# Sharing one PSUM bank between modulation columns and a K tile, an earlier normalisation, and a last tile in four pieces, in a transformer block on one core

## Chip, cores, metric

The kernel runs on one core of a Trainium2 chip (the runs came from several chips; each kernel ran next to the kernel before on the same chip). The metric is the device time of one execution in microseconds (us), the median of several runs. One run with the hardware profiler gives the trace; the span that the trace shows (first to last instruction) is about 1.8 us shorter than the time of the same run. Engines: PE multiplies matrices, PEld loads its weights, DVE and ACT work on vectors, POOL does small things, SP issues the DMAs. PSUM is the memory in which PE sums its products; this kernel uses it as eight banks of 512 columns.

## The reference

One transformer block on 2048 tokens of width 1024, cut to what matters here:

```python
mod = (silu(c) @ w_mod).reshape(1, 6, 1, -1)          # six modulation vectors from one condition vector
sa, ca, ga, sb, cb, gb = ...
h = layernorm(x) * (1 + ca) + sa                      # first modulation: needs sa and ca as columns
x = x + ga * linear_attention(h, wqkv, wo)            # q, k, v = h @ wqkv, 32 heads
h = layernorm(x) * (1 + cb) + sb
x = x + gb * ((gelu(h @ w_gate) * (h @ w_up)) @ w_down)
```

## The kernel before

Instructions are recorded in program order per engine, and semaphore waits are derived from byte ranges. Only two places matter.

The **head** is the first 39 us: nothing can be multiplied before x, the modulation weights and the K weights arrive. The first four token chunks (128 tokens each; below "first" to "fourth tokens") are normalised on DVE and transposed on PE. The modulation columns for a quarter of the width (two of the eight 128-wide slices `dc`) come from 32 one-column matmuls; DVE copies them out of PSUM and applies them; then that quarter of the K product can run. K of four chunks has eight tiles (chunk, half `jg`), each a sum of eight matmuls in a PSUM bank of its own. Seven banks are in `kb0`. The eighth tile (chunk 3, half 1) has bank 4, in which the columns are also made, so it may start only after the last copy.

```python
def mod_cols(q, bank, copy=True):                     # 4 columns, 8 matmuls each
    ...                                               # columns q*4 .. q*4+3 of the bank, start=(dc == 0)
    if copy: mod_copy(q, bank)                        # DVE: columns PSUM -> SBUF

kb0 = {(0, 0): 0, (0, 1): 1, (1, 0): 2, (1, 1): 3, (2, 0): 5, (2, 1): 6, (3, 0): 7}
...
mod_cols(0, 4, False); ...; mod_copy(0, 4); mod1(0, 1, 0, 2)   # mod1(c0, n, dc0, dc1): apply on DVE
warm(4, 7)                                            # matmuls of zeros, while waiting
k_part(0, [0])                                        # quarter 0, first tokens
ln1_bn(3, 0); mod1(1, 1, 0, 2)
k_part(0, [1])
xhat_dve(2, *xh_buf(2)); t1(2, 7)                     # third tokens: normalise, transpose, ACT copy
ln1_bn(3, 1); ln1_fin(3); mod1(2, 1, 0, 2)
warm(5)
k_part(0, [2])
xhat_dve(3, *xh_buf(3)); mod_cols(1, 4); mod1(0, 3, 2, 4); t1(3, 7)
k_part(1, [0, 1, 2]); mod1(3, 1, 0, 4); k_part(0, [3])
mod_cols(2, 4); mod1(0, 4, 4, 6)
k_part(1, [3])                                        # runs while DVE copies and applies the third columns
warm(1)
k_part(2, [0, 1, 2])
mod_cols(3, 4); mod1(0, 4, 6, 8)
k_part(2, [3])                                        # these 2 and
kv_mm(3, "k", 1, 4, list(range(6)))                   # these 6 run while DVE copies and applies the fourth
for (c_, jg), b in kb0.items():
    kv_mm(c_, "k", jg, b, [6, 7])
kv_mm(3, "k", 1, 4, [6, 7])
...                                                   # then V: (chunk, half) in the order (0,0) (1,0) | (0,1) (1,1) | ...
```

The **tail** is the last output tile. Each piece is 28 matmuls, two DVE steps and an output DMA:

```python
for k, (c0, c1) in enumerate(((0, 512), (512, 896), (896, 1024)) if last_tile else ((0, 512), (512, 1024))):
```

## Time and profile before

| what | value | where |
|---|---|---|
| time | 838.89 us, median of 3 (838.37 to 840.59); the profiled run 839.12 | times |
| span, PE busy | 837.3 us, 99% | page |
| granted clock | 1.000 | cores view |
| first columns to first V matmul ("K stage") | 9.73 to 31.46: 21.73 us | timeline of PE |
| last DVE step to end of span | 835.32 to 837.3 us | timeline |

The page of the kernel before: the span, the busy times, the clock in 40 slices, and the chain of work that ended last, by engine.

```profile
span 837.3 us, 11206 instructions
...
PE 825.8 (99%) x4081; PEld 383.3 (46%) x4160; DVE 511.5 (61%) x893; ACT 336.1 (40%) x555; POOL 37.1 (4%) x91
...
PEclk9999999999999999999999999999999999999999
...
PE 91%; DMA 4%; ACT 1%; DVE 1%; SPq 1%; issue 1%; POOL 0%; ACTq 0%; POOLq 0%
```

PE is nearly always busy and holds 91% of the chain, at full clock, so a change of order like this one can gain only at the edges of the span. The timeline of PE in the head, kernel before. Columns: start, length, engine, line, operation, names, shapes, count, and in brackets the idle time before it and what ended it. L600 makes modulation columns, L546 transposes, L680 is K (`wk`) and V (`wv`), L736 is warm-up. (A 512-wide matmul is recorded as 0.379 us long, and the next one starts 0.216 us after it; so a group's length includes 0.16 us in which its last matmul drains.)

```profile
9.73 0.95 PE L600 MATMUL ps_all<-siluT,wmq 128*128 128x1 bf16 x32 [1.33 <-DMA wmq<-in_w_mod_dram]
...
13.62 0.61 PE L546 MATMUL ps_all<-ident,xh 128*128 128x128 bf16 x8
14.06 1.24 PE L736 MATMUL ps_all<-warm 128*128 128x512 bf16 x5
15.70 1.04 PE L680 MATMUL ps_all<-wk,h1T 128*128 128x512 bf16 x4 [0.39 <-DVE h1T L565]
16.57 0.94 PE L600 MATMUL ps_all<-siluT,wmq 128*128 128x1 bf16 x32
...
21.22 0.94 PE L600 MATMUL ps_all<-siluT,wmq 128*128 128x1 bf16 x32
...
22.90 2.75 PE L680 MATMUL ps_all<-wk,h1T 128*128 128x512 bf16 x11
25.48 0.94 PE L600 MATMUL ps_all<-siluT,wmq 128*128 128x1 bf16 x32
26.29 5.34 PE L680 MATMUL ps_all<-wk,h1T 128*128 128x512 bf16 x23
31.46 3.62 PE L680 MATMUL ps_all<-wv,h1T 128*128 128x512 bf16 x16
35.46 3.61 PE L680 MATMUL ps_all<-wv,h1T 128*128 128x512 bf16 x16 [0.38 <-issue]
```

Four groups of columns start at 9.73, 16.57, 21.22 and 25.48, so the K stage has four segments, each from one group to the next: 6.84, 4.65, 4.26 and 5.98 us. Transposes of the third tokens come at 13.62, after the second tokens' K matmuls, and then PE has nothing useful until 15.70. The second V half begins at 35.46 after a wait of 0.38 us, counted from the end of the drain before it. The chain of waits of the same kernel, in order of time (start, length, what; a piece starts where the one before it ends, so here 0.17 us later than in the timeline):

```profile
25.65 0.78 PE ps_all L600 x32
26.43 1.53 PE ps_all L680 x7
...
35.08 0.38 issue
35.46 0.59 PE ps_all L680 x2
```

The tail in the timeline of DVE, kernel before: the last two pieces, 384 and 128 wide.

```profile
833.13 0.57 DVE L1135 TENSOR_TENSOR ps_all<-ps_all,gbb 128x384 f32<-128x384 f32 x1 [3.12 <-PE ps_all L1130]
...
834.69 0.30 DVE L1135 TENSOR_TENSOR ps_all<-ps_all,gbb 128x128 f32<-128x128 f32 x1 [0.41 <-PE ps_all L1130]
835.03 0.29 DVE L1137 TENSOR_TENSOR xall<-ps_all,xall 128x128 bf16<-128x128 f32 x1
```

### The profile page before, as it was taken

To read this page: it belongs to the slowest core of one execution; us is meant where nothing else is said; L and a number is where in the kernel's file an instruction comes from. 1 tells how busy PE (TensorE), PEld (TensorE's weight loads), DVE (VectorE), ACT (ScalarE), POOL (GpSimd) and SP (SyncE) were. 2 spreads that over 40 slices of the span, in tenths; PEclk is the share of its full clock that TensorE was granted. 3 is DMA by queue.
4 is the path that set the end of the run, shared out by engine and by line. 5 is a ranking of instruction groups with operands and counts; after the bars stand their busy time and mean duration, and the time that the engine had idled before them with its cause. 6 is when DMAs were issued, how large, how long until landed. Compare 5 with 4: busy or idle time off the path is not lost.

```text
span 837.3 us, 11206 instructions
## 1 busy us (share of the span) xinstructions
PE 825.8 (99%) x4081; PEld 383.3 (46%) x4160; DVE 511.5 (61%) x893; ACT 336.1 (40%) x555; POOL 37.1 (4%) x91
## 2 busy tenths in 40 slices
PE   7999999999999999999999999999999999999998
PEld 4444444444444444444444444444444444444444
DVE  6678877687785577753455665356656535655512
ACT  2357777446423354420355442045554104445300
POOL 2011111000200000010000000000000000000000
PEclk9999999999999999999999999999999999999999
DMA  9994322239696769180555533055553305555000
GB/s 286 315 253 93 109 76 74 80 81 234 145 227 207 220 203 276 30 195 26 158 151 151 151 101 75 20 158 151 151 151 101 76 20 160 153 153 144 7 19 26
DMA packets 183942, 113.22 MB, mean 135 GB/s; under 512 B 35400, under 2 KB 174920, under 8 KB 182864
## 3 DMA queue, kind: packets, MB, share of 16 engines
q1 hardware_dynamic: 183872, 112.50, 49.6%
q8 instruction: 33, 0.54, 0.3%
q14 instruction: 21, 0.17, 0.1%
q10 hardware_dynamic: 16, 0.00, 0.0%
HBM read 100.67 MB, written 4.47 MB: 126 GB/s over the span
## 4 chain that ended last, share of the span: by engine, by line
PE 91%; DMA 4%; ACT 1%; DVE 1%; SPq 1%; issue 1%; POOL 0%; ACTq 0%; POOLq 0%
PE ps_all L1130 23%; PE ps_all L1105 23%; PE ps_all L1102 21%; PE ps_all L680 13%; PE ps_all L721 7%; PE ps_all L1045 2%; DMA wu<-in_B_w_up_dram 1%; DMA h2T<-xh 1%; PE ps_all L702 1%; DMA wmq<-in_w_mod_dram 1%; DMA scr_rd<-rdc 1%; DMA rb<-scr_rd 1%; SPq L978 0%; PE ps_all L947 0%; PE ps_all L600 0%
## 5 line engine op out<-in xcount | busy, mean ns | idle before, releaser
L1105 PE MATMUL ps_all<-h2T,wu 128*128 128x512 bf16 x896 | 339.6, 379 | 1.9
L1102 PE MATMUL ps_all<-h2T,wg 128*128 128x512 bf16 x860 | 325.9, 379 | 0.0
L1130 PE MATMUL ps_all<-wd,yT 128*128 128x512 bf16 (+2 forms) x906 | 193.0, 372 | 0.9
L1113 ACT ACTIVATE q<-ps_all 128x512 f32<-128x512 f32 x112 | 66.9, 597 | 226.2 <-PE ps_all L1102 218.9
L1130 PEld LDWEIGHTS ps_all<-wd,yT 128*128 128x128 bf16 x924 | 89.2, 98 | 104.7 <-issue 0.4
L1102 PEld LDWEIGHTS ps_all<-h2T,wg 128*128 128x128 bf16 x896 | 87.7, 98 | 105.8 <-issue 0.2
L1105 PEld LDWEIGHTS ps_all<-h2T,wu 128*128 128x128 bf16 x896 | 87.7, 98 | 105.6
L1118 DVE SCALAR_TENSOR_TENSOR ww<-th,guh 128x512 f32<-128x512 f32 x112 | 77.5, 692 | 77.9 <-ACT th L1117 77.9
L1115 DVE SCALAR_TENSOR_TENSOR ww<-q,ps_all 128x512 f32<-128x512 f32 x112 | 76.9, 687 | 77.5 <-ACT guh L1114 77.4
L1117 ACT ACTIVATE th<-ww 128x512 f32<-128x512 f32 x112 | 70.5, 629 | 87.3 <-DVE ww L1115 87.3
L1135 DVE TENSOR_TENSOR ps_all<-ps_all,gbb 128x512 f32<-128x512 f32 (+2 forms) x33 | 22.5, 682 | 95.2 <-PE ps_all L1130 95.2
L1120 DVE TENSOR_TENSOR yT<-ww,ps_all 128x512 bf16<-128x512 f32 x112 | 76.9, 687 | 3.8
L1114 ACT ACTIVATE guh<-ps_all 128x512 f32<-128x512 f32 x112 | 66.3, 592 | 0.0
L680 PE MATMUL ps_all<-wk,h1T 128*128 128x512 bf16 x252 | 57.8, 379 | 1.0 <-DVE h1T L565 0.8
L680 PE MATMUL ps_all<-wv,h1T 128*128 128x512 bf16 x255 | 57.6, 379 | 0.4 <-issue 0.4
L669 ACT ACTIVATE eb<-ps_all 128x512 f32<-128x512 f32 x64 | 37.4, 600 | 48.9 <-PE ps_all L721 23.2
L721 PE MATMUL ps_all<-h1T,wq 128*128 128x512 bf16 x243 | 56.2, 379 | 0.7
L1045 PE MATMUL ps_all<-w,pq 128*128 128x512 bf16 x251 | 56.0, 379 | 0.3
L670 DVE TENSOR_SCALAR eb<-eb 128x512 f32<-128x512 f32 x64 | 27.1, 424 | 27.2 <-ACT eb L669 26.9
L1045 PEld LDWEIGHTS ps_all<-w,pq 128*128 128x128 bf16 x256 | 25.0, 98 | 30.1 <-issue 0.2
L680 PEld LDWEIGHTS ps_all<-wv,h1T 128*128 128x128 bf16 x256 | 24.9, 98 | 30.3 <-DVE eb L670 0.8
L680 PEld LDWEIGHTS ps_all<-wk,h1T 128*128 128x128 bf16 x256 | 24.5, 98 | 30.8 <-DVE h1T L565 2.3
(94 smaller groups left out, 477.1 us busy)
## 6 DMA issues: line engine op xcount, KB each, us to landing
wg<-in_B_w_gate_dram SPq DMA_DIRECT2D x56, 512.0 KB, 4.1
wu<-in_B_w_up_dram SPq DMA_DIRECT2D x56, 512.0 KB, 5.2
rb<-scr_rd SPq DMA_DIRECT2D x32, 256.0 KB, 6.9
wd<-in_B_w_down_dram SPq DMA_DIRECT2D x7, 1024.0 KB, 9.1
wmst<-in_w_mod_dram SPq DMA_DIRECT2D x6, 1024.0 KB, 6.7
wmq<-in_w_mod_dram SPq DMA_DIRECT2D x8, 512.0 KB, 7.7
out_dram<-xall SPq DMA_DIRECT2D x31, 128.0 KB, 1.7
xall<-in_A_x_dram SPq DMA_DIRECT2D x3, 1024.0 KB, 12.5
```

The lines of the kernel that those rows point to most:

```text
L680: o = sch.op(T, lambda e, dc=dc: e.matmul(PS(bank), H1[sg][:, dc, ci * P:(ci + 1) * P], W_[:, dc, jg * 512:(jg + 1) * 512], start=(dc == 0 ...
L721: o = sch.op(T, lambda e, dc=dc: e.matmul(PS(b), WQ[:, dc, qc * P:(qc + 1) * P], H1[sg][:, dc, :], start=(dc == 0), stop=(dc == NDC - 1)), ...
L1045: last[half] = sch.op(T, lambda e, g=g, half=half: e.matmul(PS(b0 + half), PQ[sg][:, g, ci * P:(ci + 1) * P], W2[:, g, half * 512:(half + ...
L1102: og = sch.op(T, lambda e, dc=dc: e.matmul(PS(bg), WG[slot][:, dc, e_ * P:(e_ + 1) * P], H2[sg][:, dc, :], start=(dc == 0), stop=(dc == ND ...
L1105: ou = sch.op(T, lambda e, dc=dc: e.matmul(PS(bu), WU[slot][:, dc, e_ * P:(e_ + 1) * P], H2[sg][:, dc, :], start=(dc == 0), stop=(dc == ND ...
L1113: sch.op(A, lambda e: e.activation(Q1[j][:, :], PS(bg), ACTF.Square, scale=math.sqrt(GELU_A)), prd=pr(bg), wr=rq, note=f"q1 {fc}")
L1114: ogh = sch.op(A, lambda e: e.activation(GUH[j][:, :], PS(bg), ACTF.Copy, scale=0.5), prd=pr(bg), wr=rg, note=f"gh {fc}")
L1115: sch.op(V, lambda e: e.scalar_tensor_tensor(WW[j][:, :], Q1[j][:, :], 1.0, PS(bg), op0=ALU.add, op1=ALU.mult), rd=rq, prd=pr(bg), wr=rw, ...
L1117: sch.op(A, lambda e: e.activation(TH[j][:, :], WW[j][:, :], ACTF.Tanh, scale=GELU_C), rd=rw, wr=rt, note=f"th {fc}")
L1118: sch.op(V, lambda e: e.scalar_tensor_tensor(WW[j][:, :], TH[j][:, :], 1.0, GUH[j][:, :], op0=ALU.add, op1=ALU.mult), rd=rt + rg, wr=rw, n ...
L1120: sch.op(V, lambda e: e.tensor_tensor(YT[:, fc, :], WW[j][:, :], PS(bu), ALU.mult), rd=rw, prd=pr(bu), wr=r_yt(fc), note=f"yT {fc}")
L1130: o = sch.op(T, lambda e, b=b, fc=fc, c0=c0, c1=c1, n=n: e.matmul(PS(b, 0, n), YT[:, fc, ci * P:(ci + 1) * P], WDT[fc // 4][:, fc % 4, c0:c1],
```

## The change

Its intent: (1) put the 16 modulation columns at the end of bank 4, so that the eighth K tile can accumulate in columns 0 to 495 of the same bank from the first quarter on (its last 16 columns come at the end, as eight 128x16 matmuls); (2) move the third tokens' normalisation and transposes ahead of the second tokens' K matmuls; (3) finer last pieces, for a shorter tail. The third-quarter K weights are also split into two loads. Core of the diff:

```diff
-            for d0, d1 in ((2 * q, 2 * q + 2),) if q < 3 else ((6, 7), (7, 8)):
+            for d0, d1 in ((2, 4),) if q == 1 else ((2 * q, 2 * q + 1), (2 * q + 1, 2 * q + 2)):
...
+        MC0 = 496                      # columns now at MC0 + q * 4 ...
-                            start=(dc == 0), stop=(dc == NDC - 1)),
+                            start=(q == t == b == dc == 0), stop=(dc == NDC - 1), skip_group_check=True),
...
+        def k31(dcs, c0=0, c1=MC0):    # eighth tile, columns c0..c1 of bank 4, start only for c0 > 0
...
         k_part(0, [0])
-        ln1_bn(3, 0)
-        mod1(1, 1, 0, 2)
-        k_part(0, [1])
         xhat_dve(2, *xh_buf(2))
         t1(2, 7)
+        mod1(1, 1, 0, 2)
+        ln1_bn(3, 0)
         ln1_bn(3, 1)
         ln1_fin(3)
+        k_part(0, [1])
         mod1(2, 1, 0, 2)
-        warm(5)
+        warm(2)
...
         k_part(0, [3])                 # k_part(q, [3]) now includes k31 of that quarter
+        k_part(1, [3])
         mod_cols(2, 4)
+        mod_copy(2, 4)
+        warm(2)
         mod1(0, 4, 4, 6)
-        k_part(1, [3])
-        warm(1)
-        k_part(2, [0, 1, 2])
+        k_part(2, [0, 1, 2, 3])
         mod_cols(3, 4)
+        mod_copy(3, 4)
         mod1(0, 4, 6, 8)
-        k_part(2, [3])
-        kv_mm(3, "k", 1, 4, list(range(6)))
         for (c_, jg), b in kb0.items():
             kv_mm(c_, "k", jg, b, [6, 7])
-        kv_mm(3, "k", 1, 4, [6, 7])
+        k31([6, 7])
+        k31(list(range(NDC)), MC0, 512)
...
-            ... ((0, 512), (512, 896), (896, 1024)) if c_ == NCH - 1 ...
+            ... ((0, 512), (512, 832), (832, 960), (960, 1024)) if c_ == NCH - 1 ...
```

More of the change, by code (lines that the diff above doesn't have):

```diff
@@ L590, in mod2, with mod_cols @@
             mods(H2, r_h2, sg, sc2, ci * P, (ci + n) * P, 0, NDC, "h2")
-        def mod_cols(q, bank, copy=True):
+        MC0 = 496
+        def mod_cols(q, bank):
             o = None
-            rng = [(bank * 2048 + q * 16, bank * 2048 + (q + 1) * 16)]
+            rng = [(bank * 2048 + (MC0 + q * 4) * 4, bank * 2048 + (MC0 + q * 4 + 4) * 4)]
             for t in range(2):
                 for b in range(2):
-                    col = q * 4 + t * 2 + b
+                    col = MC0 + q * 4 + t * 2 + b
                     for dc in range(NDC):
@@ L605, in mod_cols @@
                 sch.ps.set_writer(t_[0], t_[1], o)
-            if copy:
-                mod_copy(q, bank)
         def mod_copy(q, bank):
-            rng = [(bank * 2048 + q * 16, bank * 2048 + (q + 1) * 16)]
-            sch.op(V, lambda e: e.tensor_tensor(MODT[:, q * 4:q * 4 + 4], PS(bank, q * 4, q * 4 + 4), ADD4[:, :], ALU.add),
+            rng = [(bank * 2048 + (MC0 + q * 4) * 4, bank * 2048 + (MC0 + q * 4 + 4) * 4)]
+            sch.op(V, lambda e: e.tensor_tensor(MODT[:, q * 4:q * 4 + 4], PS(bank, MC0 + q * 4, MC0 + q * 4 + 4), ADD4[:, :], ALU.add),
                    prd=rng, rd=r_sm("add4"), wr=r_smc("modt", q, 16), note=f"modcp{q}")
@@ L751, in bass_adaLN_cond__linear_attn_block__geglu_ffn__prompt_kernel, with k_part @@
         kb0 = {(0, 0): 0, (0, 1): 1, (1, 0): 2, (1, 1): 3, (2, 0): 5, (2, 1): 6, (3, 0): 7}
-        def k_part(q, cs, dcs=(0, 1)):
-            for dc in [2 * q + k for k in dcs]:
+        def k31(dcs, c0=0, c1=MC0):
+            rng = [(4 * 2048 + c0 * 4, 4 * 2048 + c1 * 4)]
+            for dc in dcs:
+                o = sch.op(T, lambda e, dc=dc: e.matmul(PS(4, c0, c1), H1[0][:, dc, 3 * P:4 * P], WK[:, dc, 512 + c0:512 + c1],
+                                                        start=(c0 > 0 and dc == 0), stop=(dc == NDC - 1), skip_group_check=True),
+                           rd=r_h1(0, dc, dc + 1, 3 * P, 4 * P) + r_w(OFF_WK, "wk", dc, 512 + c0, 512 + c1),
+                           pwr=(rng if dc == 0 else ()), note=f"k c3 jg1 dc{dc} {c0}")
+            if dcs[-1] == NDC - 1:
+                sch.ps.set_writer(*rng[0], o)
+        def k_part(q, cs):
+            for dc in (2 * q, 2 * q + 1):
                 for (c_, jg), b in kb0.items():
@@ L757, in k_part @@
                         kv_mm(c_, "k", jg, b, [dc])
+                if 3 in cs:
+                    k31([dc])
         warm(11, 7)
@@ L769, in bass_adaLN_cond__linear_attn_block__geglu_ffn__prompt_kernel @@
         warm(6, 7)
-        mod_cols(0, 4, False)
+        mod_cols(0, 4)
         ln1_bn(2, 0)
@@ L791, in bass_adaLN_cond__linear_attn_block__geglu_ffn__prompt_kernel @@
         mod_cols(1, 4)
+        mod_copy(1, 4)
+        t1(3, 7)
         mod1(0, 3, 2, 4)
-        t1(3, 7)
         k_part(1, [0, 1, 2])
@@ L1124, in ffn_down @@
             db = 6 if ci % 2 == 0 else 4
-            for k, (c0, c1) in enumerate(((0, 512), (512, 896), (896, 1024)) if c_ == NCH - 1 else ((0, 512), (512, 1024))):
-                b = db + k if k < 2 else 0
+            for k, (c0, c1) in enumerate(((0, 512), (512, 832), (832, 960), (960, 1024)) if c_ == NCH - 1 else ((0, 512), (512, 1024))):
+                b = db + k if k < 2 else k - 2
                 n = c1 - c0
```

## The prediction

> **What bounds the kernel now.** The page gives PE 825.8 us busy of an 837.3 us span (99%), granted clock 1.000. In the chain of waits PE is 91%. After 35.5 us the timeline of PE runs to 834.67 us without a hole that this change touches. So only the first 35 us and the last 3 us are open.
>
> *Head.* The timeline shows useful PE work between 9.73 us (first modulation columns) and 31.46 us (first V matmul): 64 K matmuls at 0.216 us (13.8), 4 column groups at 0.79 (3.2), 3 token transposes at 0.46 (1.4): 18.4 us. The other 3.3 us are warm-up matmuls and waits: about 0.9 before the first K matmul, 1.5 at 14.2 to 15.7 us (third tokens late: ACT copy 1.03, then DVE), 0.5 before 18.43, 0.5 before 22.9. But DMA is at 9 tenths throughout, and landings follow each other by bytes: third and fourth columns' weights at 21.4 and 25.6 us, last K weights 26.9, the second half of the V weights about 35.4 us (issued 24.1, 11.2 us to landing). The PE wait of 0.38 us that ends at 35.46, listed as "issue", is this last DMA: PE could have gone on at 35.08.
>
> *Tail.* PE ends at 834.67; then DVE 0.31 + 0.29, then about 2 us of output DMA.
>
> **What the change does, costed.**
> - Third tokens' normalisation, transposes and ACT copy move up in front of the second tokens' K matmuls: third tokens' K matmuls start at about 14.8 instead of 15.70: -0.9 us there; three warm-ups fewer, one more later.
> - The eighth K tile loses its wait for all column copies, so it runs by quarters. It adds eight 128x16 matmuls; the 1-column ones went at 25 to 30 ns each, so +0.2 us.
> - The fourth columns now come after all third-quarter K matmuls (PE about 26.3 to 27.1, no DMA wait left), but nothing is left to fill the copy (0.16) and modulation (first piece 0.35): about 0.5 us bare wait that before was filled with eight matmuls. Roughly 0.2 to 0.6 bare before the third quarter remains.
> - Summed: K stage ends about 31.1 instead of 31.46, -0.3 us. Then PE needs the second V half: at 34.7 instead of 35.08, and still gets it at about 35.4. The bytes ahead of it are the same and splitting one weight DMA takes none away. So the 0.3 us turn into a longer wait for that DMA (0.38 to about 0.7): head gain 0, unless the landing moves.
> - Tail: pieces of 384+128 took 4.55+1.56 us; 320+128+64 take 3.80+1.56+0.81 = +0.06 us (slope 0.42 ns per column between the two forms). The Trainium skill, "TensorE: Matmul & The Clock Gate", section "Wait — 56ns, not 53.3ns?", gives 55.6 ns at 128 columns, and a floor of about 25 ns; this trace has 55.7 ns and no 64-column form. The last two DVE steps shrink from 0.30 to about 0.23 each (1.05 ns per column): -0.14. Output DMA unchanged. Net -0.1 us.
>
> **Prediction.** 838.6 us, 837.8 to 839.5; faster by 2% 0.5%, within 2% 99%, slower 0.5%.
>
> **What would show it.** Timeline of PE: third tokens' K at about 14.8; first V matmul at about 31.1; second-half V still at 35.4 with a longer wait; from there the same spacing to the end; last DVE steps near 0.23; PE end to span end about 0.1 shorter.
>
> **What would make it wrong.** The second V half landing earlier (then up to 0.6 us gain) or later (the extra DMA shifts which DMA each later issue waits for; then a loss); a column group waiting for its weights now that PE comes earlier; 64-column matmuls slower than 29 ns because weight loads no longer hide; 128-byte output rows landing later.

## More of the kernel before

L702 is the first K-V product, which needs V of the first tokens.

After the fourth columns (25.48) K matmuls follow at once (26.29).

## The result

The changed kernel took 838.88 us (median of 6, 838.56 to 839.24); the kernel before, on the same chip, 838.38 (median of 6, 838.08 to 840.59). The ratio is 1.0002, 95% interval 0.9989 to 1.0014. Ratios here are the mean time of one kernel's fast runs over that of the other's in the same rounds, so not quite the ratio of the medians. The kernel before now and then takes 839.9 to 840.7 us (5 of the 39 of its runs), and those pull its mean up. Three of the five list a mean granted clock of 0.998 instead of 1.000, which by itself would make 0.002 x 838.6 = 1.7 us; one (839.90) lists 1.000, and for one (840.59) no clock is on record. Medians are the better guide below: 838.60 over those 39 runs, 839.08 over 11 runs of the changed kernel (6 here, 5 in a repeat). The changed kernel is about 0.5 us, or 0.06%, slower. The interval of the ratio includes 1, in the repeat too (0.9993 to 1.0018), so this rests on the medians and on the traces below.

The page of the changed kernel, the lines that answer to those before:

```profile
span 836.8 us, 11359 instructions
...
PE 830.2 (99%) x4194; PEld 384.4 (46%) x4194; DVE 511.7 (61%) x895; ACT 336.1 (40%) x555; POOL 37.1 (4%) x91
...
PE 98%; DMA 1%; DVE 1%; SPq 0%; ACT 0%; issue 0%
```

The span of this profiled run is 0.5 us shorter than that of the profiled run before, while the medians go the other way. One profile each is not enough for half a microsecond. (No reading rests on PE's share of the chain, 91% and 98%: it is 97% in a second profile of the kernel before.) The timeline of PE, changed kernel (L602 makes columns, L756 is the eighth tile):

```profile
9.20 0.95 PE L602 MATMUL ps_all<-siluT,wmq 128*128 128x1 bf16 x32 [0.59 <-DMA wmq<-in_w_mod_dram]
...
14.27 1.04 PE L680 MATMUL ps_all<-wk,h1T 128*128 128x512 bf16 x4 [0.17 <-DVE h1T L565]
15.14 0.94 PE L602 MATMUL ps_all<-siluT,wmq 128*128 128x1 bf16 x32
...
21.06 0.94 PE L602 MATMUL ps_all<-siluT,wmq 128*128 128x1 bf16 x32
21.86 0.59 PE L736 MATMUL ps_all<-warm 128*128 128x512 bf16 x2
22.71 1.69 PE L680 MATMUL ps_all<-wk,h1T 128*128 128x512 bf16 x7 [0.25 <-DVE h1T L565]
...
26.16 0.94 PE L602 MATMUL ps_all<-siluT,wmq 128*128 128x1 bf16 x32
27.81 3.30 PE L680 MATMUL ps_all<-wk,h1T 128*128 128x512 bf16 x14 [0.71 <-DVE h1T L565]
...
31.57 7.07 PE L680 MATMUL ps_all<-wv,h1T 128*128 128x512 bf16 x32
38.47 0.62 PE L702 MATMUL ps_all<-vs,pk 128*128 128x129 bf16 x8
```

The third tokens' K matmuls (14.27) come 5.07 us after the first columns instead of 5.97: the gain of 0.9 us is there. But the third columns start at 21.06 and the third-quarter K matmuls only at 22.71, and the fourth columns start at 26.16 and the fourth-quarter matmuls at 27.81. The segments are 5.94, 5.92, 5.10 and 5.41: 22.37 us, 0.64 more than before. The first V matmul starts at 31.57, although the first columns came 0.53 us earlier in this execution. From there 32 V matmuls run without a wait for the second V half. The chain of waits behind the fourth columns, changed kernel:

```profile
26.32 0.79 PE ps_all L602 x32
...
27.14 0.17 DVE modt L611
...
27.34 0.42 DVE h1T L565
...
27.81 3.30 PE ps_all L680 x14
```

Before, K matmuls stood at this place in the chain. Now the chain leaves PE for the copy (0.17) and the first application (0.42). Seen from PE, it issues nothing useful from 26.95 (26.16 plus 32 column matmuls, 0.79) to 27.81: 0.86 us. Those are 0.16 of drain, 0.17 of copy, 0.42 of application, and 0.1 of hand-overs.

The tail of the changed kernel, DVE:

```profile
831.95 0.50 DVE L1149 TENSOR_TENSOR ps_all<-ps_all,gbb 128x320 f32<-128x320 f32 x1 [2.38 <-PE ps_all L1144]
...
834.33 0.23 DVE L1149 TENSOR_TENSOR ps_all<-ps_all,gbb 128x64 f32<-128x64 f32 x1 [0.19 <-PE ps_all L1144]
834.59 0.23 DVE L1151 TENSOR_TENSOR xall<-ps_all,xall 128x64 bf16<-128x64 f32 x1
```

The last two DVE steps take 0.23 us instead of 0.30 and 0.29.

### The profile page after: what moved, and what is told of

Its sections match the earlier page's. It is cut to its first block, busy times and chain, and to the rows that moved or that the text cites. A ratio compares the mean times of both kernels' runs of the same rounds, so it can differ in the third digit from the quotient of the medians.

```text
span 836.8 us, 11359 instructions
## 1 busy us (share of the span) xinstructions
PE 830.2 (99%) x4194; PEld 384.4 (46%) x4194; DVE 511.7 (61%) x895; ACT 336.1 (40%) x555; POOL 37.1 (4%) x91
## 3 DMA queue, kind: packets, MB, share of 16 engines
HBM read 100.67 MB, written 4.47 MB: 126 GB/s over the span
## 4 chain that ended last, share of the span: by engine, by line
PE 98%; DMA 1%; DVE 1%; SPq 0%; ACT 0%; issue 0%
PE ps_all L1144 23%; PE ps_all L1116 23%; PE ps_all L1119 23%; PE ps_all L680 13%; PE ps_all L1059 7%; PE ps_all L721 7%; PE ps_all L702 1%; DMA wmq<-in_w_mod_dram 1%; PE ps_all L961 0%; PE ps_all L602 0%; DVE h1T L565 0%; PE ps_all L973 0%; PE ps_all L756 0%; PE ps_all L643 0%; SPq L442 0%; DVE st L742 0%
## 5 line engine op out<-in xcount | busy, mean ns | idle before, releaser
L1116 PE MATMUL ps_all<-h2T,wg 128*128 128x512 bf16 x896 | 339.6, 379 | 0.0
L1144 PE MATMUL ps_all<-wd,yT 128*128 128x512 bf16 (+3 forms) x952 | 194.2, 366 | 0.0
L1149 DVE TENSOR_TENSOR ps_all<-ps_all,gbb 128x512 f32<-128x512 f32 (+3 forms) x34 | 22.7, 667 | 94.8 <-PE ps_all L1144 94.8
L721 PE MATMUL ps_all<-h1T,wq 128*128 128x512 bf16 x256 | 58.7, 379 | 0.0
```

Of the source, the lines that this page charges most:

```text
L721: o = sch.op(T, lambda e, dc=dc: e.matmul(PS(b), WQ[:, dc, qc * P:(qc + 1) * P], H1[sg][:, dc, :], start=(dc == 0), stop=(dc == NDC - 1)), ...
L1116: og = sch.op(T, lambda e, dc=dc: e.matmul(PS(bg), WG[slot][:, dc, e_ * P:(e_ + 1) * P], H2[sg][:, dc, :], start=(dc == 0), stop=(dc == ND ...
L1144: o = sch.op(T, lambda e, b=b, fc=fc, c0=c0, c1=c1, n=n: e.matmul(PS(b, 0, n), YT[:, fc, ci * P:(ci + 1) * P], WDT[fc // 4][:, fc % 4, c0:c1],
```

## The experiments

Two theories at the start. **A**: the order of work on PE sets the time of the head; the changed kernel lost its filler behind the third and fourth columns, and the 0.38 us wait in the profile before was one execution's late load. **B** (that of the prediction): the second V half's DMA sets the time of both. A third, **D**, comes up with the parts: the weight DMAs pace the columns, so an earlier PE only waits for them. Each kernel ran five times or six, next to the kernel before on the same chip, with one profile each. All outputs were correct.

The segments in all profiles, in us. "V asked" is when PE would start on the second V half (first V matmul plus 16 x 0.216); "V landed" is from the landing records of the trace. Both are on the clock of the span.

| kernel | 1st to 2nd columns | to 3rd | to 4th | to first V | K stage | V landed / asked | median time (before beside it) |
|---|---|---|---|---|---|---|---|
| before | 6.84 | 4.65 | 4.26 | 5.98 | 21.73 | 35.4 / 34.9 | 838.89 |
| before again | 6.84 | 4.65 | 4.25 | 5.98 | 21.72 | 31.9 / 34.8 | 838.60 (838.61) |
| changed | 5.94 | 5.92 | 5.10 | 5.41 | 22.37 | 34.0 / 35.0 | 838.88 (838.38) |
| changed again | 5.98 | 5.92 | 5.09 | 5.42 | 22.41 | 32.6 / 35.6 | 839.18 (838.61) |
| tail only | 6.88 | 4.65 | 4.35 | 5.98 | 21.86 | 33.8 / 34.8 | 838.80 (838.61) |
| third tokens up only | 5.97 | 4.65 | 4.47 | 5.98 | 21.07 | 33.7 / 34.5 | 838.07 (838.62) |
| eighth tile only | 6.83 | 5.91 | 5.10 | 5.40 | 23.24 | 33.3 / 36.4 | 840.06 (838.62) |
| filler behind 4th columns | 6.58 | 5.91 | 4.24 | 5.41 | 22.14 | 32.9 / 35.1 | 838.34 (838.61) |
| filler behind 3rd and 4th | 5.97 | 5.49 | 4.23 | 5.41 | 21.10 | 32.8 / 33.7 | 837.58 (838.62) |
| the same again | 6.92 | 5.49 | 4.23 | 5.41 | 22.05 | 32.9 / 35.5 | 838.10 (838.58) |
| all but the eighth tile | 5.97 | 4.65 | 4.24 | 5.98 | 20.84 | 32.0 / 34.0 | 837.65 (838.58) |
| third tokens, tail, V order | 5.97 | 4.65 | 4.90 | 5.98 | 21.51 | 33.2 / 36.2 | 838.66 (838.62) |
| before, late V half | 6.85 | 4.64 | 4.25 | 5.98 | 21.72 | 35.7 / 35.3 | 839.66 (838.53) |
| changed, late V half | 6.08 | 5.92 | 5.09 | 5.41 | 22.50 | 35.7 / 35.7 | 839.60 (838.53) |

The two odd first segments (6.58, 6.92) belong to executions in which the first K weights landed late: the first K matmul came 2.76 and 3.11 us after the first columns, instead of 2.14 to 2.27 in the other rows. In both, the landing records have these weights 0.14 us before that matmul (12.10 and 12.96 us). (For the version with another V order, "asked" is eight matmuls later.)

From the first V matmul to the end of the span, the profiles without a wait in the V stage agree: 805.31 us with three tail pieces, 805.21 to 805.22 with four (times from the packed trace, which has three decimals). So the span is the start of the first columns, the K stage, and this constant. The first columns start when their weights land, and that differs between executions of one kernel (9.73 and 9.65 us before, 9.20 and 9.76 changed). This is why K stages can be compared between single profiles and whole spans can't.

### Both kernels again

> The kernel before, unchanged, against itself: ratio 1.000, and its spread is the noise of the comparison. Theory A (the PE order sets the time; the profile of before fell on an execution with late weights): the second V half lands at about 34 us as in the profile after, the first V matmul starts at about 31 and no wait stands before the second V half; span about 836.6. Theory B (the second V half's DMA sets the time of both kernels): it lands at about 35.4 again and PE waits for it again.

> The changed kernel, unchanged. Theory A: the K stage, from the first modulation columns to the first V matmul, takes about 22.4 us again, 0.6 more than in before (21.7), no wait for the second V half, and the time is 0.3 to 0.6 us above before. Theory B: the time equals before within 0.1, and the second V half lands when PE asks for it or later.

The kernel before, repeated: the timeline of PE at the start of V.

```profile
31.37 7.07 PE L680 MATMUL ps_all<-wv,h1T 128*128 128x512 bf16 x32
38.27 0.62 PE L702 MATMUL ps_all<-vs,pk 128*128 128x129 bf16 x8
```

The 32 V matmuls run through: 6.90 us from the first V matmul to the first K-V product, against 7.45 in the first profile, so there the late load cost 0.55 us (the 0.38 idle and the 0.16 of drain). The second V half had landed at 31.9. Before took 838.60 (838.61 beside it), the changed kernel 839.18. Theory A's numbers hold (K stage 21.72 and 22.41, difference 0.69, time 0.57). In this pair both kernels found the load landed, so theory B can't set the difference.

### The tail alone

```diff
-  ... ((0, 512), (512, 896), (896, 1024)) if c_ == NCH - 1 ...
+  ... ((0, 512), (512, 832), (832, 960), (960, 1024)) if c_ == NCH - 1 ...
```

> The kernel before with only the last output tile in four pieces. By the costs read from the trace: PE end 0.06 us later, last two DVE steps 0.14 shorter: 0.1 us faster than before, the head unchanged. Rival: the tail is what costs the 0.4 us (smaller output rows land later): then this kernel is 0.3 to 0.5 us slower than before, and the time from the last DVE step to the end of the span grows.

The time (838.80 against 838.61) is too coarse for 0.1 us, and its sign was missed. The trace resolves it: from the first K-V product to the end of the last DVE step 796.35 us, against 796.41 in both profiles of before; from there to the end of the span 1.97, against 2.00 in both. The tail gains 0.10 us, as expected, and the rival (smaller output rows cost 0.4) falls.

### Filler behind the fourth columns

The first build put the eighth tile's matmuls behind the fourth columns as filler, as the kernel before had done (there they come after two matmuls of another bank and wait for the copy). PE would write bank 4 while DVE reads the columns out of it, and nothing orders the two. The Trainium skill, "PSUM — Partial Sum Buffer", section "PSUM bank collisions raise a hardware error", says why this counts even with disjoint columns: two engines may not touch one bank in the same 32 partitions at once. No run here shows it. So the filler was taken from tiles in other banks:

```diff
-        k_part(2, [0, 1, 2, 3])
+        k_some(2, [(0, 0), (0, 1), (1, 0), (1, 1), (2, 0)])
+        k31([4, 5])
         mod_cols(3, 4)
         mod_copy(3, 4)
+        k_some(2, [(2, 1), (3, 0)])
         mod1(0, 4, 6, 8)
```

> The changed kernel with four third-quarter K matmuls (tiles that are not in the shared bank) moved from in front of the fourth columns to behind them, so that PE has work while the columns are copied and applied. Theory A: the bare 0.7 us before the fourth-quarter matmuls goes, first V matmul 0.7 us earlier relative to the first columns, and the time falls by 0.6 to 0.7 us against the changed kernel. Theory B: the 0.7 us reappear as a wait before the second V half and the time is that of the changed kernel within 0.15.

```profile
26.20 0.94 PE L602 MATMUL ps_all<-siluT,wmq 128*128 128x1 bf16 x32
27.00 4.15 PE L680 MATMUL ps_all<-wk,h1T 128*128 128x512 bf16 x17
```

In the timeline of PE the 17 K matmuls recorded after the fourth columns (26.20) start at once (27.00). The third segment falls by 0.85 us, from 5.09 to 4.24 (four matmuls moved out of it), and the fourth stays at 5.41, since the four now stand where PE had been idle. The K stage of this profile fell by only 0.27 because its first K weights landed late. The time fell by 0.84, from 839.18 to 838.34, somewhat more than the 0.6 to 0.7 that A expected. B expected no change.

### The parts alone

Third tokens moved up in the kernel before, nothing else (the `xhat_dve` to `warm(2)` hunk of the diff):

> The kernel before with only the third tokens' normalisation moved up (and three warm-ups fewer). Theory A (segments add): first to second columns 6.84 to about 6.0 us, the other three segments as before, K stage 20.9 instead of 21.7, time 0.8 us below before (about 837.8). Theory D (the weight DMA paces the columns, so an earlier PE only waits for it): the 0.85 us come back as waits at the third and fourth columns, K stage 21.5 to 21.7, time as before.

First segment 5.97 (A), but the third grew by 0.22: an earlier PE met the third-quarter weights not yet landed ("DMA wk<-in_A_wqkv_dram: 0.2"). K stage 21.07, time 0.55 below before. So A is right for three quarters of it, and D for the rest.

The eighth tile's part alone (the changed kernel with that hunk and the tail put back; the split load stays in):

> The changed kernel with the third tokens' normalisation back at its old place and the tail in three pieces: the eighth tile's part alone. Theory A: second to fourth segments as in the changed kernel, first as in before: K stage 23.2 to 23.3, time 1.4 to 1.5 us above before (about 840.1). Rival (the eighth tile by quarters is neutral or helps, the loss lies in the other parts): time at or below before.

```profile
22.45 0.94 PE L602 MATMUL ps_all<-siluT,wmq 128*128 128x1 bf16 x32
...
24.10 1.68 PE L680 MATMUL ps_all<-wk,h1T 128*128 128x512 bf16 x7 [0.25 <-DVE h1T L565]
...
27.55 0.94 PE L602 MATMUL ps_all<-siluT,wmq 128*128 128x1 bf16 x32
29.52 2.98 PE L680 MATMUL ps_all<-wk,h1T 128*128 128x512 bf16 x13 [1.03 <-DVE h1T L565]
```

The timeline of PE shows both holes: third columns at 22.45 and K at 24.10; fourth columns at 27.55 and K at 29.52, with 13 of the 14 matmuls of that group on record, so its first one, at about 29.2 by the hole of the changed kernel, is probably missing from the trace. K stage 23.24, time 1.44 above before: as A expected. The interval of the ratio (1.0003 to 1.0028) excludes 1.

### Filler behind both columns, and a reordered V stage

```diff
-        k_part(1, [3])
+        k31([2, 3])
         mod_cols(2, 4)
         mod_copy(2, 4)
-        warm(2)
+        k_some(1, [(3, 0)])
```

> The changed kernel with filler behind the third columns as well as the fourth (two matmuls that are not in the shared bank behind the third). Theory A: third to fourth columns about 0.4 shorter than in the fourth-only version, minus any wait for the third columns' weights; K stage about 21.2, time 0.2 to 0.4 below the fourth-only version and 0.4 to 0.6 below before. Theory D: third columns now wait for their weights and nothing is gained over the fourth-only version.

K stage 21.10, 837.58 us, 1.04 below before, more than the 0.4 to 0.6 expected. The K stage (0.62) and the tail (0.10) explain 0.7 of it; the rest isn't explained.

> The version with filler behind the third and fourth columns, a second time: K stage 21.1 again, time 1.0 us below before (0.8 to 1.2) and PE asking for the second V half at about 24.5 us after the first columns, without a wait for it.

The repeat gave 838.10, 0.48 below before and less than the 0.8 to 1.2 expected, with runs from 837.62 to 839.02. Its profile fell on the slowest one, in which the first K weights landed 3.0 us after the first columns began. The median of its ten runs is 837.63.

A version with the V order changed, on top of the third tokens and the tail:

```diff
-  ... (((0, 0), (1, 0)), ((0, 1), (1, 1)), ((2, 0), (2, 1)), ((3, 0), (3, 1)))[c_]
+  ... (((0, 0), (1, 0)), ((2, 0), (0, 1)), ((1, 1), (2, 1)), ((3, 0), (3, 1)))[c_]
```

> A version meant to beat both: before, with the third tokens moved up, the tail in four pieces, and the V stage taking a third first-half tile ahead of the second half, so that PE asks for the late half 1.7 us later. Theory A: 0.8 + 0.06 us under before (about 837.7), and no execution with a wait before the second V half. Theory D: as before, less 0.06.

It failed: 838.66, no better than before. Its list of waits has a line that the others lack (who waited for whom: us, times, longest):

```profile
PE ps_all L702 <- ACT vs L693: 0.5, 1, 0.5
```

A second line stands in the timeline of its PE, in the middle of the third columns:

```profile
21.02 0.55 PE L600 MATMUL ps_all<-siluT,wmq 128*128 128x1 bf16 x16 [0.35 <-DMA wmq<-in_w_mod_dram]
```

The V tile (0, 1) now comes right before the first K-V product that needs it, and that product waits for ACT's copy. From the first V matmul to the end of the span this profile takes 805.85 us, 0.64 more than the others with four tail pieces. So the remedy for a rare wait put another in its place (one profile was taken). The rest of the loss is theory D again: the third columns waited 0.35 us for their weights, the third-quarter K weights came late too (0.2), and the K stage is 21.51, 0.67 longer than in the next experiment, which has the same order of work up to V but splits the third-quarter load.

### All but the eighth tile

Third tokens up, split third-quarter loads and four tail pieces, with the columns and the eighth tile as before:

> The whole change without its eighth-tile part: third tokens moved up, third-quarter weights in two loads, four tail pieces; the eighth tile and the column bank as in before. Theory A: segments about 6.0, 4.65, 4.25, 6.0: K stage 20.9 (the 0.2 us wait for the third-quarter weights of the version with the third tokens alone goes), time 0.7 to 0.9 us below before, 1.3 to 1.5 below the changed kernel. Rival (the parts work only together): time at or above that of the version with the third tokens alone, -0.55.

```profile
24.58 0.94 PE L600 MATMUL ps_all<-siluT,wmq 128*128 128x1 bf16 x32
25.39 5.34 PE L680 MATMUL ps_all<-wk,h1T 128*128 128x512 bf16 x23
30.56 7.07 PE L680 MATMUL ps_all<-wv,h1T 128*128 128x512 bf16 x32
```

The timeline of PE: fourth columns at 24.58, K matmuls from 25.39, V at 30.56, no hole. The 0.2 us wait of the third tokens alone is gone (third segment 4.24). That the split removed it isn't shown: in this profile all the third-quarter weights had landed by 21.47 us, before PE began with them at 21.98, and in the other they landed at 22.37. K stage 20.84 and 837.65 us, 0.93 below before (interval of the ratio 0.9974 to 0.9999) and, each taken against the kernel before on its own chip, about 1.4 below the changed kernel. It beats both, by as much as the version with filler does, and without the shared bank.

### The prediction's regime, made on purpose

The second V half was loaded after the next 1 MB of x, in both kernels:

```diff
-        w_dma(WV, OFF_WV, "wv", 2, 512, 1024)
         x_dma(4, 8)
+        w_dma(WV, OFF_WV, "wv", 2, 512, 1024)
```

> The kernel before with the second V half loaded after the next 1 MB of x instead of ahead of it, so that it lands when that x did, at 34.7 to 38 us. This makes the regime that the prediction assumed. If the wait in the profile of before was that load, a wait stands before the second V half's first matmul (about 34.8) until the landing, 0.2 to 2 us, and the time rises by as much above before. Rival (the wait was something else, a bank or an engine): no new wait.

> The changed kernel with the same late load. If the load caps both, the changed kernel's longer K stage (22.4 instead of 21.7) is hidden in a shorter wait, and the time is that of the late version of before within 0.3 us, less than the 0.5 to 0.6 between the kernels as they are. Rival: the 0.5 to 0.6 stay.

The timeline of PE, kernel before with the late load:

```profile
31.82 3.62 PE L680 MATMUL ps_all<-wv,h1T 128*128 128x512 bf16 x16
35.78 3.61 PE L680 MATMUL ps_all<-wv,h1T 128*128 128x512 bf16 x16 [0.34 <-issue]
```

The changed kernel with the late load:

```profile
32.27 7.09 PE L680 MATMUL ps_all<-wv,h1T 128*128 128x512 bf16 x31
39.20 0.62 PE L702 MATMUL ps_all<-vs,pk 128*128 128x129 bf16 x8
```

The load landed at 35.7 in both profiles. The kernel before would have asked at 35.3, and waited, listed as "issue" as in its first profile; the changed kernel asked at 35.7 and hardly waited (0.02 us). The first K-V product comes at 39.23 and 39.20, although the K stages are 21.72 and 22.50. So the wait is that load, and where it lands late, it hides the difference in K stages. The times, 839.66 and 839.60 (beside 838.53), agree with this, but the runs of each kernel spread over 1.8 us. The rise of 1.1 us is more than the wait, which cost 0.5 us in the profile (7.41 instead of 6.91 from the first V matmul to the first K-V product); the rest isn't explained. The mechanism of the prediction exists, in a regime that the kernels as they are seldom enter.

## Why the prediction was right or wrong

The time (838.88) lies in the range (837.8 to 839.5) and "within 2%" was right. The direction wasn't: it expected 0.3 us less than 838.89, and the medians say 0.5 us more. (The three runs behind 838.89 also stood 0.3 above the kernel's median, so part of the expected gain was never there.) That the time fell into the range is luck as far as the mechanism goes: the range is 1.7 us wide, and the K stage was forecast 0.3 us shorter and came out 0.69 longer.

- *"Third tokens' K matmuls start at about 14.8 instead of 15.70: -0.9 us there"*: right. The first segment is 0.86 to 0.90 shorter with this part alone and in the whole change.
- *"Eight 128x16 matmuls ... +0.2 us"*: agrees with the trace. Two 496-wide and these eight take 0.60 us in the chain of waits, of which two 496-wide are 0.42. The floor of about 25 ns per matmul that the Trainium skill, "TensorE: Matmul & The Clock Gate", section "Wait — 56ns, not 53.3ns?", states shows in this trace: the one-column matmuls and the 16-wide ones start 25 ns apart.
- *"About 0.5 us bare wait that before was filled with eight matmuls"*: the term that failed. The hole is 0.86 us, drain and hand-overs included. After taking out the work itself (columns 0.79, wide matmuls 0.216 each, the small ones 0.2 together), the fourth segment has 0.99 us bare, against 0.01 before: the hole, and 0.13 more, which fits the wait of the next matmuls for the second application (their weight load waits for it).
- *"Roughly 0.2 to 0.6 bare before the third quarter remains"*: it was entered as no change. Before it was 0.44 with the filler of two matmuls; now it is 0.86 of the third segment: +0.42.
- *"Summed: K stage ends about 31.1 ..., -0.3 us"*: wrong by these two. -0.86 + 0.42 + 0.98 + 0.15 (the small matmuls less the narrower wide ones) = +0.69, which is the measured 22.41 - 21.72.
- *"So the 0.3 us turn into a longer wait for that DMA ... head gain 0"*: the step that failed in reasoning. It read a wait in one execution as the limit of all. In the 12 profiles with the normal load order PE waited for that load once. The experiments with the late load show that the cause of that wait was named rightly.
- *"Tail: net -0.1 us"*: right. The constant after the first V matmul is 805.31 us with three pieces and 805.21 with four: 0.06 up to the last DVE step, about 0.03 after it. The 64-wide matmuls came 29.1 ns apart by their records, as estimated.

The sum: +0.69 in the K stage and -0.10 in the tail make +0.59 expected from traces, against +0.5 in the medians. Why the kernel before sometimes takes 839.9 us and more, and why three of these runs had the lower clock, is left open; no such run fell into a profile.

## What to carry to other kernels

When work is moved from behind a short dependent chain to in front of it, the chain's full length comes into view: price it from the last matmul's start through drain, copy, application and hand-overs (0.86 us here), not by its two DVE instructions alone. A tile that shares a bank with what another engine is about to read can't serve as filler while that read is pending, so sharing a bank to start a tile sooner may take away the very filler that hid the copy. A wait in a single profile says what limited that execution; before building an argument on a load's landing time, look at the same load in a second profile.

## What the Trainium skill lacked or had wrong

- "TensorE: Matmul & The Clock Gate", section "Back-to-back issue gap": it gives about 81 ns (128 columns) and 131 ns (512 columns) per matmul for streams in which each matmul loads its weights, and calls the isolated formula, columns / 2.4 + 2.5, wrong for them. Here each matmul of the last output tile has its own weight load, and they started 55.9 ns (128 columns), 29.1 ns (64) and 215.8 ns (512) apart: the formula, not the figures for streams.
- No page that was read gives the length of the round trip from PE through two small DVE steps back to PE; here it is 0.86 us, of which the DVE instructions are 0.59 (0.17 + 0.42).
- "DMA: Bandwidth & Descriptors" was not found to say how far the landing of one load moves between executions of the same kernel: the second V half landed at 31.9 and at 35.4 us (9.2 and 11.2 us after its issue) in two executions of the kernel before.
